# Attention, token mixer and gated mixer in one kernel: three engines in program order from batch 2 on, and the first token product behind the second channel product

## Chip, cores and metric

One core of one Trainium2 chip. The metric is the device time of one execution in microseconds (us). Engines: PE is TensorE, ACT is ScalarE, DVE is VectorE, POOL is GpSimd, SP is SyncE, which here only issues DMAs.

## The reference

Eight batches of 576 tokens, model width 512. Per batch:

```python
# attention in chunks of 64 tokens, 8 heads of 64
attn = softmax(q_c @ k_c.T / 8);  x = attn @ v_c            # x: 576 x 512
# token and channel mixer
u = x + (relu(x.T @ w_tok1) @ w_tok2).T                      # d_tok 256
x = u + relu(u @ w_ch1) @ w_ch2                              # d_ch 1536
# gated mixer
h = relu(x @ w_in);  a, v = h[:, :512], h[:, 512:]
v = (v - mean(v)) / sqrt(var(v) + 1e-6)                      # over features
out = (a * (w_spatial @ v + b_spatial)) @ w_out
```

## The kernel before

Each float32 operand is held as two float16 parts, a high one and the remainder ("hi" and "lo"), and each product is three products, hi x hi, hi x lo and lo x hi, in one PSUM accumulation. ScalarE rounds to the high part, VectorE or GpSimd subtracts for the remainder. That rounding, ReLU, residuals, statistics and softmax keep the other engines at work beside TensorE.

A batch `b` runs through these stages on TensorE: the first channel product (`ch1`, from batch 2 on `ch1_fast`), the second (`ch2`, from batch 3 on `ch2_fast`), the gate stage (`gate_v` for five token tiles and `gate` for four feature tiles, in turns), then for batch b+1 the token products `tok1` and `tok2`, then `gated`, the spatial product of batch b. The output projection `proj` of batch b is issued in the next batch, between pairs of the channel product. Attention of batch b+2 is put between all these in small steps: `at_steps` lists them for a group of 128 tokens (five groups a batch), `pump`, called after each matrix product, keeps a planned TensorE clock, and `a_step` runs the next step when a slower clock, scaled stage by stage with `PACES`, reaches its due time. `a_until(b + 1)` ahead of `tok1` runs what is left for batch b+1.

The fast channel products (batches 2 to 7, `ch1_fast`; 3 to 7, `ch2_fast`) are a Strassen-like form with seven block products in place of eight. The weight blocks and their sums are made once (`sum_steps`, batches 1 and 2), stored to HBM and streamed through 18 slots. `ch1_fast` goes in pairs p = 0 to 5; after each pair VectorE, ScalarE and GpSimd form seven operands `hF[p]` for the second channel product (lines 707 to 749). `ch2_fast` begins with `p1(0)`, `p1(1)`, `p2(0)`: `p2` adds to a PSUM bank that ScalarE must first have copied at L779.

PSUM is four buffers of two banks (`pm`), taken by every product in turn. `wrk` has three work tiles of 128 x 576.

The first part of the program, ahead of the loop over batches, has its order written out by hand. In the loop only TensorE's order is that of the program; ScalarE, VectorE, GpSimd and SP are ordered by the planner of the framework from its own cost estimates, with `tc.high_priority()` around the steps that are to come first. Each engine takes its instructions strictly in the order that results.

Of the kernel before, what the change touches and what calls it, by code (L numbers as in the profile page):

```python
# [1 line left out]

# [24 lines left out]
def mixer_kernel(ctx: ExitStack, tc, qk0, qk, v, wt1, wt2, wc1, wc2, win, wsp, bsp, wout, out):  # L27
# [10 lines left out]
    wrk = ctx.enter_context(tc.tile_pool(name="wrk", bufs=3))  # L38
# [4 lines left out]
    pm = ctx.enter_context(tc.tile_pool(name="pm", bufs=4, space=bass.MemoryType.PSUM))  # L43

# [176 lines left out]
    def at_steps(g):  # L221
# [12 lines left out]
        def score():  # L234
            m["sp"] = sp = pm.tile([128, 2, 512], F32, tag="m", name="mp")
            for h in range(4):
                for k, (x, y) in enumerate(THREE):
                    for r in range(2):
                        for c in range(nc_):
                            t = slice(64 * c, 64 * c + 64)  # L240
                            PE.matmul(out=sp[t, r, 64 * h:64 * h + 64], lhsT=qk16[half[r], x, 0, h, t],  # L241
                                      rhs=qk16[half[r], y, 1, h, t], start=(k == 0), stop=(k == 2))

        def shift():
            sc = m["sp"][rows, :, 0:256].rearrange("p r (h k) -> p r h k", k=64)
            mx = sm.tile([128, 2, 4, 1], F32, name="mx")
            m["sd"] = sd = sdp.tile([128, 4, 2, 64], F32, name="sd")
            DVE.tensor_reduce(out=mx[rows], in_=sc, axis=AX.X, op=ALU.max)
            DVE.tensor_tensor(out=sd[rows].rearrange("p h r k -> p r h k"), in0=sc,
                              in1=mx[rows].to_broadcast([n, 2, 4, 64]), op=ALU.subtract)  # L250
# [3 lines left out]

        def norm():
            sd = m["sd"][rows].rearrange("p h r k -> p (h r) k")
            mx = sm.tile([128, H, 1], F32, name="mx")
            DVE.tensor_reduce(out=mx[rows], in_=sd, axis=AX.X, op=ALU.add)
            DVE.tensor_scalar(out=mx[rows], in0=mx[rows], scalar1=1e-9, scalar2=None, op0=ALU.add)
            DVE.reciprocal(out=mx[rows], in_=mx[rows])  # L260
            DVE.tensor_tensor(out=sd, in0=sd, in1=mx[rows].to_broadcast([n, H, 64]), op=ALU.mult)  # L261
# [16 lines left out]
        def attend():  # L278
            m["av"] = av = pm.tile([128, 2, 512], F32, tag="m", name="mp")
# [25 lines left out]
        def x_lo():  # L305
# [3 lines left out]
        return [  # L309
            [lambda: at_load_qk(g)], [], [qk_hi], [qk_lo], [], [score],  # L310
            [lambda: wide_v(b, 2 * i, vals)],
            [shift], [], [expo], [norm, v_hi], [p_hi, v_lo], [p_lo], [], [], [attend], [x_out],
            [], [x_lo], [],
        ]


# [19 lines left out]
    def wide_steps(g):  # L336
# [11 lines left out]
        def score():  # L348
# [4 lines left out]
            m["sp"] = sp = pm.tile([128, 2, 512], F32, tag="m", name="mp")  # L353
# [33 lines left out]
        def attend():  # L387
            m["av"] = av = pm.tile([128, 2, 512], F32, tag="m", name="mp")
# [29 lines left out]
    KA, NA = 5, 20  # L418
    live = {}
    order = sorted((KA * g + s + 15 * (g >= 2 * NT), g, s) for g in range(NT, NG) for s in range(NA))  # L420
    todo = [0]

    def a_step():
# [4 lines left out]
        with tc.high_priority() if g < 2 * NT and s not in (0, 8) else nullcontext(), tc.issue_after(mark) if g < 2 * NT else nullcontext():  # L428
            for f in live[g][s]:
                f()  # L430

    def a_end(b):
        return [o[1:] for o in order].index((NT * b + NT - 1, NA - 1)) + 1
# [8 lines left out]
    pumps = []  # L442

    def pump(cols):
        t = cols / 2.4 + 2.5
        clock[0] += t
        slow[0] += t * pace[0]
        for p in pumps:
            while p[3]() and p[4][0] >= p[0]:
                p[2]()  # L450
                p[0] += p[1]
# [10 lines left out]
    def psum2():  # L462
        t = pm.tile([128, 2, 512], F32, tag="m", name="mp")
        return [t[:, 0, 0:288], t[:, 1, 0:288]], t[:, :, 0:288]

    def psum1():
        t = pm.tile([128, 2, 512], F32, tag="m", name="mp")
        return t[:, 0, :]
# [30 lines left out]
    def behind():  # L499
        stack = ExitStack()  # L500
        for ins in tail.values():
# [3 lines left out]
    PACES = ({"first": 0.2, "pair": 0.8, "ch1": 1.0, "ch2": 1.3, "gate": 1.0, "tok1": 1.0, "last": 0.3},  # L505
             {"first": 0.0, "pair": 0.2, "ch1": 1.0, "ch2": 1.95, "gate": 1.85, "tok1": 1.5, "last": 0.0})
# [7 lines left out]
    def first_sums(ps, m, x):  # L514
# [4 lines left out]
        split(x[:, m, s], xb[:, 0, m, s], xb[:, 1, m, s])  # L519
# [5 lines left out]
        if m == 3:  # L525
            q1, q2, q3 = sums[0], wrk.tile([128, 2, 288], F32, tag="t", name="q2"), wrk.tile([128, 2, 288], F32, tag="t", name="q3")
            DVE.tensor_tensor(out=q2, in0=b22, in1=q1, op=ALU.subtract)
            split(q2, tq[1][:, 0], tq[1][:, 1], POOL)
            DVE.tensor_tensor(out=q3, in0=b22, in1=b12, op=ALU.subtract)
            split(q3, tq[2][:, 0], tq[2][:, 1], POOL)  # L530
            DVE.tensor_tensor(out=q1, in0=b21, in1=q2, op=ALU.subtract)
            split(q1, tq[3][:, 0], tq[3][:, 1], POOL)
# [72 lines left out]
    def sum_steps(stage, p, room):  # L605
        rv = room.bitcast(F32)
        f = rv[:, 0:1024].rearrange("p (k m) -> p k m", k=4)
        s = rv[:, 1024:2048].rearrange("p (n k m) -> p n k m", n=4, k=2)
        g = room[:, 0:2048].rearrange("p (n e k m) -> p n e k m", n=4, e=2, k=2)
        if stage == 1:  # L610
            w = c1w[:, :, p]
            a11, a12, a21, a22 = f[:, 0:2, 0:128], f[:, 2:4, 0:128], f[:, 0:2, 128:256], f[:, 2:4, 128:256]
        else:
            w = c2w[:, :, 2 * p:2 * p + 2].rearrange("p e k (h m) -> p e (k h) m", h=2)
            a11, a12, a21, a22 = f[:, 0:2, 0:128], f[:, 2:4, 0:128], f[:, 0:2, 128:256], f[:, 2:4, 128:256]

        def join():
            DVE.tensor_tensor(out=f, in0=w[:, 0], in1=w[:, 1], op=ALU.add)
            for n, (k, c) in ((A11, (0, 0)), (A12, (2, 0)), (A22, (2, 128))):
                for e in range(2):  # L620
# [3 lines left out]
                    else:  # L624
                        at = (p // 2) * 512 + e * 256 + p % 2 * 128
                        SP.dma_start(out=c2s[:, n, :, at:at + 128].rearrange("q p m -> p q m"), in_=w[:, e, k:k + 2, c:c + 128])
# [12 lines left out]
        def low():  # L639
# [3 lines left out]
            else:  # L643
                at = (p // 2) * 512 + p % 2 * 128
                for q in range(2):
                    for e in range(2):
                        SP.dma_start(out=c2s[q, 3:7, :, at + e * 256:at + e * 256 + 128].rearrange("n p m -> p n m"), in_=g[:, :, e, q])

        return [join, first, second, high, low]
# [3 lines left out]
    def sum_next():  # L653
        with behind():
# [22 lines left out]
    def new_bank():  # L677
        return pm.tile([128, 2, 512], F32, tag="m", name="mp")

# [4 lines left out]

    def ch1_fast(full, between):
        high = tc.high_priority
        ab, cd = {}, {}

# [7 lines left out]
        def store(c, hi, lo, eng=POOL):  # L696
            ACT.activation(out=c, in_=c, func=AF.Relu)
            split(c, hi, lo, eng)

        for p in range(7):  # L700
            pace[0] = PACE["first" if p < 1 else "pair"]
            if p < 6:
                ab[p] = a = new_bank()
                product(a[:, 0], p, A11, xb[:, :, 0:2, T1], True)
                product(a[:, 1], p, S2, tq[1], True)
                with high():
                    ACT.activation(out=s1b[0], in_=a[:, 0, 0:288], func=AF.Copy)
                    DVE.tensor_tensor(out=u2b[p % 2], in0=a[:, 1, 0:288], in1=s1b[0], op=ALU.add)
            if p:
                d, u, xp = cd[p - 1], u2b[(p - 1) % 2], xs[(p - 1) % 2]  # L710
                product(d[:, 0], p - 1, S4, xb[:, :, 2:4, T2], False)
                product(d[:, 1], p - 1, A22, tq[3], False)
                with high():
                    c = new_work("c")
                    DVE.tensor_tensor(out=c, in0=d[:, :, 0:288], in1=spread(u), op=ALU.add)  # L715
                    if full:
                        f = hF[p - 1]
                        ACT.activation(out=xp[:, 1:4:2], in_=c, func=AF.Relu)
                        t13, t24 = new_work("t13"), new_work("t24")
                        relu_less = dict(scalar=0.0, op0=ALU.max, op1=ALU.subtract)  # L720
                        DVE.scalar_tensor_tensor(out=t13[:, 0], in0=c[:, 0], in1=xp[:, 0], **relu_less)
                        DVE.tensor_tensor(out=t24[:, 0], in0=xp[:, 2], in1=t13[:, 0], op=ALU.subtract)
                        DVE.scalar_tensor_tensor(out=t24[:, 1], in0=c[:, 1], in1=t24[:, 0], **relu_less)
# [430 lines left out]
```

## Time and profile before

| what | value |
|---|---|
| median of 3 runs | 1176.37 us (1174.98 to 1178.49) |
| profiled execution | 1176.0 us, span 1174.0 us |
| PE busy | 1100.7 us, 94% |
| DVE, ACT, POOL busy | 771.0, 501.8, 424.5 us |
| mean granted TensorE clock | 0.98 |

The span runs from the first to the last instruction of the profiled execution. Busy time is the union of an engine's instructions. A matrix product counts from its start to its modelled end, so products overlap and a busy TensorE isn't one at its peak. A releaser ("<-") is the instruction whose end let a waiting one start.

### The profile page before, as it was taken

The numbers are of one execution on the slowest core, as the hardware profiler recorded it, in microseconds if no ns is written. First come the engines' busy times: TensorE is split into PE (matmuls) and PEld (weight loads), VectorE is DVE, ScalarE is ACT, GpSimd is POOL, SyncE is SP. The second block draws the span as 40 slices with busy tenths as digits, with TensorE's granted clock in tenths as the row PEclk, the third lists the DMA queues.
The fourth block names the chain that finished last, engine by engine and source line by source line (L and its number), as shares of the span: only waits on it lengthen the run. The fifth ranks groups of instructions, "written<-read, shape, count | busy, mean of one in ns | idle before, by whom it ended". The sixth has DMA issues, their size and how long they took to land.

```text
span 1174.0 us, 26626 instructions
## 1 busy us (share of the span) xinstructions
PE 1100.7 (94%) x10860; PEld 774.0 (66%) x10860; DVE 771.0 (66%) x1299; ACT 501.8 (43%) x884; POOL 424.5 (36%) x392
## 2 busy tenths in 40 slices
PE   5898999999999999999799897998979999999998
PEld 4576757776577755766467574675746767677765
DVE  7999886765565487574666756667576675467342
ACT  3343444434345344453444634356243553346131
POOL 0000033352344445453335623346234452345221
PEclk9899999999999999999999998999989999999999
DMA  9488720654046442356514585145751469115401
GB/s 318 141 250 268 230 53 20 147 160 124 18 125 169 92 121 50 110 144 186 147 32 118 139 198 133 40 118 139 203 132 27 127 166 199 19 55 153 135 1 45
DMA packets 191819, 148.36 MB, mean 126 GB/s; under 512 B 107345, under 2 KB 175697, under 8 KB 189393
## 3 DMA queue, kind: packets, MB, share of 16 engines
q1 hardware_dynamic: 191696, 146.66, 45.8%
q8 instruction: 85, 1.39, 0.5%
q14 instruction: 38, 0.30, 0.1%
HBM read 112.00 MB, written 20.45 MB: 113 GB/s over the span
## 4 chain that ended last, share of the span: by engine, by line
PE 62%; DVE 20%; DMA 5%; ACT 5%; issue 3%; POOL 3%; SPq 1%; ACTq 0%; DVEq 0%; POOLq 0%
PE mp L669 23%; PE mp L457 22%; PE mp L939 5%; PE mp L862 4%; PE mp L836 3%; PE mp L480 3%; DVE gb L154 2%; DVE gb L150 1%; DMA qk<-in_qk 1%; DVE qk L232 1%; DVE gb L148 1%; DVE c L715 1%; PE mp L241 1%; DMA c2s<-vn 1%; DVE sd L261 1%
## 5 line engine op out<-in xcount | busy, mean ns | idle before, releaser
L669 PEld LDWEIGHTS <-c1w 128*128 128x128 f16 x2772 | 272.1, 99 | 94.3 <-issue 19.1
L669 PE MATMUL mp<-xb,c1w 128*128 128x288 f16 x864 | 127.4, 287 | 8.1 <-DVE c2w L749 6.7
L836 PE MATMUL mp<-hb,c2w 128*128 128x288 f16 x864 | 111.7, 288 | 4.2 <-DVE c2w L163 2.7
L457 PE MATMUL mp<-xb,inw 128*128 128x288 f16 x768 | 104.9, 296 | 9.5 <-ACT hb L921 8.9
L457 PE MATMUL mp<-spw,vn 128*128 128x288 f16 x896 | 111.6, 286 | 0.0
L457 PEld LDWEIGHTS <-inw 128*128 128x128 f16 x768 | 77.4, 101 | 38.0 <-issue 11.8
L457 PEld LDWEIGHTS <-vn 128*128 128x128 f16 x896 | 87.4, 98 | 22.8
L836 PEld LDWEIGHTS <-c2w 128*128 128x128 f16 x864 | 83.4, 99 | 27.5 <-DVE c2w L163 4.0
L669 PE MATMUL mp<-hb,c1w 128*128 128x288 f16 x630 | 91.8, 291 | 8.5 <-ACT vn L779 7.3
L939 PE MATMUL mp<-otw,gb 128*128 128x512 f16 x432 | 98.0, 379 | 0.0
L862 PE MATMUL mp<-inw,xb 128*128 128x512 f16 x384 | 91.6, 381 | 5.9 <-ACT xb L544 2.5
L669 PE MATMUL mp<-c2w,c1w 128*128 128x288 f16 x630 | 92.3, 292 | 0.0
L457 PE MATMUL mp<-xb,c1w 128*128 128x288 f16 x576 | 74.9, 290 | 4.4 <-DVE xb L538 2.5
L939 PEld LDWEIGHTS <-gb 128*128 128x128 f16 x432 | 42.3, 98 | 45.5
L457 PEld LDWEIGHTS <-c1w 128*128 128x128 f16 x576 | 56.2, 99 | 20.5 <-issue 2.9
L862 PEld LDWEIGHTS <-xb 128*128 128x128 f16 x384 | 36.1, 98 | 47.2 <-ACT xb L544 3.5
L669 PE MATMUL mp<-c1w 128*128 128x288 f16 x432 | 66.1, 288 | 0.0
L929 POOL TENSOR_TENSOR gb<-gt,gb 128x576 f16<-128x576 f32 x31 | 41.1, 1327 | 66.0 <-ACT gb L928 66.0
L545 POOL TENSOR_TENSOR xb<-rt,xb 128x576 f16<-128x576 f32 x7 | 11.7, 1676 | 140.3 <-ACT xb L544 140.3
L895 POOL TENSOR_TENSOR vn<-vt,vn 128x512 f16<-128x512 f32 x32 | 37.8, 1183 | 61.9 <-ACT vn L894 61.9
L269 POOL TENSOR_TENSOR p<-sd,p 128x512 f16<-128x512 f32 (+1 forms) x30 | 39.5, 1318 | 56.7 <-ACT p L266 54.8
L886 POOL TENSOR_TENSOR y<-z,mhalf 128x1 f32<-128x1 f32 (+1 forms) x40 | 24.1, 603 | 89.9 <-DVE z L885 86.2
(233 smaller groups left out, 1993.4 us busy)
## 6 DMA issues: line engine op xcount, KB each, us to landing
c1w<-c1s SPq DMA_DIRECT2D x252, 128.0 KB, 2.4
c1w<-c2s SPq DMA_DIRECT2D x210, 128.0 KB, 2.5
qk<-in_qk SPq DMA_DIRECT2D x96, 128.0 KB, 3.0
out<-o SPq DMA_DIRECT2D x31, 256.0 KB, 2.1
v<-in_v SPq DMA_DIRECT2D x56, 128.0 KB, 3.0
vn<-in_wc SPq DMA_DIRECT2D x4, 1024.0 KB, 4.9
otw<-in_wc SPq DMA_DIRECT2D x3, 1024.0 KB
spw<-in_wc SPq DMA_DIRECT2D x3, 1024.0 KB, 5.0
```

Source lines behind the costliest of these rows:

```text
L148: DVE.tensor_scalar(out=t, in0=w[:, :, 1], scalar1=3, scalar2=0x3FFFFFFF, op0=ALU.logical_shift_left, op1=ALU.bitwise_and)
L154: DVE.scalar_tensor_tensor(out=t, in0=w[:, :, 0], scalar=29, in1=t, op0=ALU.logical_shift_right, op1=ALU.bitwise_or)
L269: POOL.tensor_tensor(out=p_hl[rows, 1], in0=m["sd"][rows], in1=p_hl[rows, 0], op=ALU.subtract)
L457: PE.matmul(out=o, lhsT=l, rhs=r, start=(i == 0), stop=(i == len(seq) - 1))
L480: PE.matmul(out=pss[m], lhsT=l, rhs=r, start=(i + j == 0), stop=False)
L669: PE.matmul(out=o[:, 0:288], lhsT=w[:, a, k], rhs=b(e, k), start=(start and k + i == 0), stop=(stop and k == 1 and i == 2), skip_group_che ...
L836: PE.matmul(out=o, lhsT=c2w[:, a, k, mc], rhs=hb[:, k // 2, r, k % 2 * 2 + t], start=(k + e == 0), stop=(k == 11 and e == 2))
L862: PE.matmul(out=ps, lhsT=l, rhs=r, start=(k + e == 0), stop=(k == 3 and e == len(seq) - 1))
L886: POOL.tensor_tensor(out=y[0:n], in0=z[0:n], in1=mhalf[0:n], op=ALU.pow)
L895: POOL.tensor_tensor(out=vn[:, 2 * j + 1], in0=t, in1=vn[:, 2 * j], op=ALU.subtract)
L929: eng.tensor_tensor(out=gl, in0=t, in1=gh, op=ALU.subtract)
L939: PE.matmul(out=ps, lhsT=gb[:, l, k, tk], rhs=otw[:, r, k], start=(k == 0 and e == 0), stop=(k == 3 and e == 2))
```

## The change

From batch 2 on, ScalarE, VectorE and GpSimd also follow the order of the program (`ordered.enter_context`, `exact[0] = True`). SP stays with the planner. So that the program's order is usable, dependent steps are not issued where they stand but some microseconds of TensorE's planned clock later: `after(us, f)` pushes `f` on a heap, `tick` in `pump` runs what is due; ahead of batch 2 `after` runs `f` at once. `tok1` of batch b+1 moves from behind the gate stage to directly behind the second channel product of batch b (`next_tokens`), with attention of batch b+1 ended ahead of it and that of b+2 begun behind it; `tok2` stays. Attention's step list becomes times on one axis, ten units between groups; score and attend products wait for a minimum distance from the steps that feed them (`BEHIND`, `held`), and the pace table becomes three tables with other values. The sums for the second channel weights go from six whole to twelve half pieces, in `xs[0]`, spread over batch 2. A fifth projection moves into the first channel product, the gate tiles' order changes, `wrk` gets a fourth tile.

```diff
-    wrk = ctx.enter_context(tc.tile_pool(name="wrk", bufs=3))
+    wrk = ctx.enter_context(tc.tile_pool(name="wrk", bufs=4))
...
-        return [
-            [lambda: at_load_qk(g)], [], [qk_hi], [qk_lo], [], [score],
...
-        ]
+        return {0: lambda: at_load_qk(g), 4: qk_hi, 5.5: qk_lo, 10: score, 10.2: lambda: wide_v(b, 2 * i, vals), 11: top, 11.8: shift,
+                14: expo, 16: total, 17.5: norm, 18.8: v_hi, 19: p_hi, 19.8: v_lo, 20.5: p_lo, 28: attend, 29: x_out, 30.5: x_lo}
...
-    order = sorted((KA * g + s + 15 * (g >= 2 * NT), g, s) for g in range(NT, NG) for s in range(NA))
+    order = sorted((5 * g + s, g, s) for g in range(NT, 2 * NT) for s in range(20))
+    order += sorted((10 * g + s, g, s) for g in range(2 * NT, NG) for s in TIMES)
...
+    BEHIND = {10: (5.5, 3000.0), 28: (20.5, 7000.0)}
+
+    def a_open():
+        _, g, s = order[todo[0]]
+        if not exact[0] or s not in BEHIND:
+            return True
+        s0, gap = BEHIND[s]
+        return not held[0] and clock[0] >= told[g, s0] + gap
...
+    def after(us, *fs):
+        for f in fs:
+            if exact[0]:
+                heappush(jobs, (clock[0] + 1000 * us, after.count, f))
+                after.count += 1
+            else:
+                f()
...
-    PACES = ({"first": 0.2, "pair": 0.8, "ch1": 1.0, "ch2": 1.3, "gate": 1.0, "tok1": 1.0, "last": 0.3},
-             {"first": 0.0, "pair": 0.2, "ch1": 1.0, "ch2": 1.95, "gate": 1.85, "tok1": 1.5, "last": 0.0})
+    SPAN = 102000.0
+    PACES = ({"first": 0.2, "pair": 0.8, "ch1": 1.0, "ch2": 1.3, "gate": 1.0, "tok1": 1.0, "last": 0.3, "turn": 0.8},
+             {"first": 0.0, "pair": 1.1, "ch1": 1.0, "ch2": 1.7, "gate": 1.2, "tok1": 1.0, "last": 0.0, "turn": 0.9},
+             {"first": 0.0, "pair": 0.7, "ch1": 1.0, "ch2": 1.75, "gate": 1.45, "tok1": 1.0, "last": 0.0, "turn": 0.3})
...
+            after(0.7, second)
+            after(1.3, lambda: put(xp[:, 2:4], 1))
+            after(1.6, others)
+            after(3.0, lambda: put(t13, 3))
+            after(3.6, lambda: put(t24, 5))
...
+        start = 0.8 if j < 4 else 2.2
+        after(start, spread_of)
+        after(start + 2.0, newton)
+        if exact[0]:
+            after(start + 2.2, finish)
+            return None
         return finish
...
+            if b == FIRST_FAST:
+                ordered.enter_context(tc.manual_schedule(engines={ET.Activation, ET.DVE, ET.Pool}))
+                exact[0] = True
+                sum_pump([(2, p, q) for p in range(6) for q in range(2)], 1550.0)
...
+            def next_tokens():
+                a_until(b + 1)
+                pumps[:] = pumps[1:]
+                pace[0] = PACE["tok1"]
+                last = tok1()
+                attention_from(b + 2, 0.0, 112000.0 if b < 1 else SPAN)
+                return last
+
+            if exact[0] and b < B - 1:
+                next_tokens()
```

In `sums_of` (new, called after each pair) the five `after` lines place the sums and splits of lines 721 to 727; `put` is ScalarE's rounding and GpSimd's remainder. `others` holds the sums of lines 723 and 724. The residuals' copies (`tail_copy`), `first_sums`, `gated` and the half tile of `gate_v` get `after` in the same way.

## Rows read from the trace of the kernel before

**Rows 1.** windows, batches 2 to 6: stretch, us, engines' busy us, clock, DMA share, GB/s

```profile
337.30:477.90 140.60, 135.80 (x1278) 94.92 (x1276) 85.27 (x138) 61.17 (x109) 68.77 (x68) 0.99 0.42 108
477.90:623.10 145.20, 133.98 (x1326) 93.11 (x1324) 93.37 (x167) 65.61 (x120) 60.77 (x53) 0.95 0.47 125
623.10:769.60 146.50, 134.79 (x1338) 93.41 (x1337) 94.59 (x167) 66.49 (x123) 60.28 (x53) 0.97 0.49 126
769.60:913.50 143.90, 132.52 (x1327) 92.24 (x1325) 94.60 (x167) 65.49 (x120) 60.89 (x53) 0.96 0.48 126
913.50:1046.50 133.00, 129.91 (x1243) 91.13 (x1242) 82.93 (x151) 59.98 (x115) 56.54 (x51) 1.00 0.47 115
```

**Rows 2.** windows: channel 2, gate (batch 4), gate (6), channel 2 (7)

```profile
668.00:705.40 37.40, 35.12 (x422) 26.86 (x421) 21.15 (x37) 13.46 (x24) 13.47 (x13) 0.95 0.74 181
705.40:740.80 35.40, 28.51 (x322) 17.07 (x320) 23.65 (x50) 15.56 (x27) 11.58 (x14) 0.90 0.50 129
...
993.00:1017.70 24.70, 24.70 (x246) 15.62 (x246) 14.85 (x39) 11.18 (x21) 10.10 (x12) 1.00 0.31 46
...
1087.90:1118.70 30.80, 30.80 (x253) 24.61 (x252) 9.11 (x19) 4.91 (x10) 7.72 (x8) 1.00 0.39 117
```

**Rows 3.** waits of TensorE, whole span: us in total, times, longest

```profile
PE mp L241 <- ACT vt L872: 9.1, 3, 3.6
PE mp L457 <- ACT hb L921: 8.9, 3, 3.1
...
PE mp L669 <- ACT vn L779: 7.3, 4, 2.3
PE mp L669 <- DVE c2w L749: 6.7, 3, 2.2
PE mp L457 <- ACT hb L487: 3.9, 8, 2.1
...
PE mp L862 <- ACT xb L544: 2.5, 2, 1.8
...
PE mp L862 <- DVE xb L545: 1.6, 2, 1.4
```

**Rows 4.** timeline of TensorE, batch 4: start, us, instructions, idle before

```profile
674.83 1.31 PE L669 MATMUL mp<-hb,c1w 128*128 128x288 f16 x9 [2.28 <-ACT vn L779]
675.93 2.36 PE L669 MATMUL mp<-c2w,c1w 128*128 128x288 f16 x9
...
730.85 4.60 PE L457 MATMUL mp<-xb,inw 128*128 128x288 f16 x24 [2.69 <-ACT hb L921]
735.28 2.75 PE L862 MATMUL mp<-inw,xb 128*128 128x512 f16 x12
737.87 3.10 PE L457 MATMUL mp<-xb,inw 128*128 128x288 f16 x24
```

**Rows 5.** timeline of VectorE, batch 4, turn between the channel products

```profile
667.20 1.48 DVE L261 TENSOR_TENSOR sd<-sd,mx 128x512 f32<-128x512 f32 x1
668.61 0.74 DVE L715 TENSOR_TENSOR c<-mp,vn 128x576 f32<-128x576 f32 x1
```

**Rows 6.** timeline of ScalarE, batch 3, gate stage

```profile
585.05 0.63 ACT L894 ACTIVATE vn<-vt 128x512 f16<-128x512 f32 x1 [3.06 <-DVE vt L891]
585.58 0.63 ACT L921 ACTIVATE hb<-mp 128x576 f32<-128x576 f32 x1
```

**Rows 7.** groups by line, VectorE: count, busy us, mean ns, idle before

```profile
L724 DVE TENSOR_TENSOR t<-vn 128x288 f32<-128x288 f32 x15 | 16.4, 1096 | 0.0
...
L749 DVE SCALAR_TENSOR_TENSOR c2w<-mp,c2w 128x288 f16<-128x288 f32 x15 | 6.7, 444 | 0.0
```

**Rows 8.** DMA issues; columns: count, median us to landing

```profile
x<-xh SPq DMA_TRANSPOSE x24, 3.3
```

**Rows 9.** groups by line, GpSimd

```profile
L306 POOL TENSOR_TENSOR xh<-xT,xh 128x512 f16<-128x512 f32 x24 | 28.1, 1170 | 42.8 <-ACT xh L303 23.8 <-PE mp L241 9.1 <-issue 9.0
```

More of the change, by code (lines that the diff above doesn't have):

```diff
@@ L234, in score @@
         def score():
[L235 removed]
+            m["sp"] = sp = bank()
             for h in range(4):
@@ L447, in pump, with tick @@
         slow[0] += t * pace[0]
+        tick()
+    def tick():
+        while jobs and jobs[0][0] <= clock[0]:
+            heappop(jobs)[2]()
         for p in pumps:
@@ L644, in low @@
                 at = (p // 2) * 512 + p % 2 * 128
[L645 to L649, printed above, removed]
+                for e in range(2):
+                    SP.dma_start(out=c2s[q, 3:7, :, at + e * 256:at + e * 256 + 128].rearrange("n p m -> p n m"), in_=g[:, :, e])
+        return [join, first, second, high, low] + [lambda: None] * (stage > 1)
     todo_sums = []
     def sum_next():
-        with behind():
+        with nullcontext() if exact[0] else behind():
             todo_sums.pop(0)()
@@ L992, in mixer_kernel, with when @@
         wticks[0] = KW * 5 + 1
-    with tc.manual_schedule(engines={mybir.EngineType.PE}):
+    with tc.manual_schedule(engines={ET.PE}), ExitStack() as ordered:
         def attention_from(b, skip, span):
             if b < B:
-                end = a_end(b)
-                pumps.append([slow[0] + skip, span / (end - todo[0]), a_step, lambda: todo[0] < end, slow])
+                end, base, first = a_end(b), slow[0] + skip, order[todo[0]][0]
+                unit = span / (order[end - 1][0] - first)
+                def when():
+                    at = [order[min(i, end - 1)][0] for i in (todo[0] - 1, todo[0])]
+                    return max(base + (at[1] - first) * unit, slow[0] + (at[1] - at[0]) * unit * 0.6)
+                pumps.append([base, span / (end - todo[0]) if b < 3 else when, a_step, lambda: todo[0] < end and a_open(), slow])
         def held_tick():
@@ L1023, in mixer_kernel @@
                 full = b >= FIRST_FULL
-                places = (1, 3, 5, 6) if full else (2, 5)
-                early, pend = pend[:len(places)], pend[len(places):]
-                ch1_fast(full, {k: (lambda i=i: proj(b - 1, i)) for k, i in zip(places, early)})
-            pace[0] = PACE["ch2"]
+                ch1_fast(full, {k: (lambda i=i: proj(b - 1, i)) for k, i in zip((5, 2, 4, 1, 3), pend)})
+                pend = []
+            pace[0] = PACE["ch2" if b < FIRST_FULL else "turn"]
             if b == 0:
@@ L1074, in mixer_kernel @@
             if b < B - 1:
-                a_until(b + 1)
-                pumps[:] = pumps[1:]
-                pace[0] = PACE["tok1"]
-                last = tok1()
-                attention_from(b + 2, 0.0, 112000.0)
+                if not exact[0]:
+                    last = next_tokens()
                 if b == 0:
@@ L1094, in mixer_kernel @@
                 pend = list(range(5 if b % 2 else 4))
-        banks = [t[:, a] for t in [pm.tile([128, 2, 512], F32, tag="m", name="mp") for _ in range(3)] for a in range(2)]
+        settle()
+        banks = [t[:, a] for t in [bank() for _ in range(3)] for a in range(2)]
         for ks in ((0, 1), (2,)):
```

256 lines of the change are left out of this document (137 added, 119 removed).

## The prediction

> **What bounds the kernel now.** I read the batches first, as stretches of the trace cut at the end of each batch's spatial product [rows 1]. TensorE is the busiest engine in every batch, so time is lost where it stops or runs slowly. Batches 3, 4 and 5 take 145.2, 146.5 and 143.9 us, batch 6 takes 133.0 with about as many matrix products. The reader is to see that the long ones have less PE share and a granted clock of 0.95 to 0.97, where batch 6 has 1.00, and that no other engine is near full: VectorE, the next one, has 94.6 of 146.5 us.
>
> The stages of batch 4 [rows 2] say where. The second channel product takes 37.4 us against 30.8 us in batch 7, where there is no attention beside it. The gate stage takes 35.4 us against 24.7 us in batch 6, where TensorE never stops. VectorE is busy 23.65 us in the long gate stage and 14.85 us in the short one: the difference is attention.
>
> Then the waits of TensorE [rows 3]. Few kinds make up nearly all from batch 2 on, and they come at the same places of each batch: a score product waits for a PSUM bank that ScalarE empties (9.1 us), a gate product for the next bank (8.9), the second channel product for ScalarE's copy of its first sum (7.3), a first channel product for VectorE's remainder (6.7), `tok2` for the hidden layer of `tok1` directly ahead of it (3.9), the gate stage for the last residual (2.5 and 1.6).
>
> The timeline of TensorE [rows 4] shows what a wait costs beyond itself. Behind the 2.28 us wait that ends at 674.8 us nine products take 1.31 us, and then the next nine 2.36; behind the wait that ends at 730.9 us 24 take 4.60 us, and the next such 24 take 3.10. The clock column of [rows 2] is 0.95 and 0.90 in just these stages, so part of them ran at the lower of the two levels, 1.2 GHz.
>
> Last, the engines that are waited for. At 667.2 us VectorE runs a normalisation of attention (1.48 us) while the channel sums of the last pair, which begin at 668.6 us, stand behind it [rows 5]; ScalarE's copies for those sums come late, and the short copy that TensorE needs stands behind them. In the gate stage ScalarE waits 3.06 us with the rounding of `vn` at the head of its queue, for a VectorE result, and only then does the 0.63 us that empties a bank for TensorE [rows 6]. So TensorE waits not for capacity but for work that is in the wrong place in an in-order queue.
>
> **The change part by part.** *Order of three engines.* No arithmetic goes away. `after` puts a dependent step later in program text by a time on TensorE's planned clock: the remainders, Newton steps and roundings no longer stand ahead of the copies that free a bank. `finish` of a gate tile comes 3.0 us after its product, while the next gate product is 24 x 0.123 = 2.9 us long [rows 4], so the emptying of that bank stands ahead of it in ScalarE's queue. The wait of [rows 6] has no place there. In the turn from the first to the second channel product the last split is put 3.6 us later, behind the first copy.
>
> What can be won is the sum of the waits that the order makes [rows 3]:
> - gate stage, 9.1 + 8.9 = 18.0;
> - turn into the second channel product, 7.3;
> - inside the first channel product, 6.7;
> - residual to gate, 2.5 + 1.6 = 4.1;
> - `tok1` to `tok2`: 3.9 in eight waits, the longest 2.1, so the others about 0.26; three of those lie ahead of batch 2, which leaves 3.1.
>
> That is 39.2 us. A wait also costs the filling of the array: nine products take 1.31 us, which is eight distances of 0.123 us and one of 0.3, so about 0.17 is lost at each of some 22 waits, 3.7 us. The slow clock is bounded from both sides. From below: two slow stretches a batch in 3, 4 and 5 and two in batch 2, eight at the 1.5 us of 4.60 against 3.10, 12 us. From above: one minus the clock times the length of batches 2 to 5 [rows 1], 1.4 + 7.3 + 4.4 + 5.8 = 18.9, which counts the waits themselves as slow. I take 13, near the lower end, as the rows 4 are direct. All together 56 us, at most 62.
>
> How much is kept? The residual wait and the `tok2` wait I count as gone (7.2): the first is at most 1.8 us long [rows 3] and gets 28 products of 512 columns as cover, 6 us by the 2.75 us for twelve [rows 4]; the second gets the whole gate stage between. If that cover is gone, the same 7.2 us come back. Gate waits: VectorE had 8.8 us of attention there, and the pace of attention in this stage goes from 1.85 to 1.45, so 14.85 + 6.9 = 21.7 us of VectorE work meet 24.7 us of TensorE. That is 88%, too close to lose no time in a fixed order; a quarter stays, 4.5 us. Of the turn and the first channel product (14.0) a sixth stays, 2.3. Of filling and clock (16.7) a sixth, 2.8.
>
> *`tok1` behind the second channel product.* It asks for two PSUM buffers while the last two of the channel product are being emptied. No row shows this wait; below it is nothing, above it is 1.8 us a batch (the longest wait for that residual), and below nothing it can't be, as a bank is never freed earlier by it. Nearest is the wait of 0.26 us; I take 0.2 us, 1.0 for five batches. What is late next is `tok1` itself, if attention isn't through (rival four).
>
> *Attention.* 17 steps in place of 20, ten units from group to group, paced so that it ends before the second channel product does; its products are held until 3.0 and 7.0 us behind the steps that feed them. Its loads and transposes move with it on SP's queue, whose order the planner still chooses; I count nothing, between a gain and a loss of 0.5 us a batch. *Sums for the second channel weights*: spread over batch 2 in twelve halves. 48 small GpSimd instructions in place of 24; even if each new one cost the 1.17 us of a full tile [rows 9], GpSimd would rise from 68.8 to 97 us in a batch of some 130 [rows 1]: hidden. *Fifth projection* moved into the first channel product and a fourth work buffer: nothing, same products, no wait in [rows 3] on either. Batches 0 and 1 are still planned; their planned order shifts a little, nothing within 2 us.
>
> Sum: 55.9 - 4.5 - 2.3 - 2.8 - 1.0 = 45.3 us. The profiled execution took 1176.0 us around a span of 1174.0, and the median of the runs is 1176.37, so one is as good as the other: **1131 us**.
>
> **Rivals.** *One: everything is recovered.* 1176 less 56 to 62, 1114 to 1120; I count below 1116. For it: batch 6 runs at clock 1.00 under the old order already. Against: it has less attention.
>
> *Two: VectorE and GpSimd hold each other.* The same VectorE difference of two SBUF operands takes 1.10 us on average, a form with one PSUM operand 0.44 us [rows 7]. The hand order puts splits on GpSimd at fixed times (1.3, 3.0, 3.6 us) and the sums between (0.7, 1.6). If four sums a pair each lose 0.66 us, a pair needs 2.6 us more of VectorE; with two pairs of a batch that have no projection to hide it, that is 5 us in each of five batches, 25 us given back, and the time is 1156; with one such pair 1144. Against: the 1.6 us sums come before the first split can start. The Trainium skill (SBUF — State Buffer, Who interferes with whom) says that a VectorE instruction with two SBUF inputs contends with a GpSimd one that reads SBUF and that the second to issue waits for the whole of the first. By that rule it would be about 1156; the 1.10 us rows agree with it, though no row shows which engine came first.
>
> *Three: transfers bind.* The second channel product streams weights at a DMA share of 0.74 in 37.4 us; in 33 us that is 0.84 [rows 2]. If late weights hold the stage at its old length in batches 3 to 6, the turn's 7.3 us and four slow stretches (6.0) aren't won: 1144. Against: 0.84 is under 1 and the stage starts with 18 slots loaded.
>
> *Four: attention isn't ready for `tok1`, slower than before.* `tok1` used to come behind the gate stage; now all five groups must be in token order by the end of the second channel product. A last group that is still at its normalisation owes 1.5 us [rows 5], two GpSimd steps of 1.2 [rows 9], two transposes of 3.3 [rows 8], its products (some 0.6) and two copies of 0.6 [rows 6]: 12.3 us with TensorE idle, five times 62 us, 1176 - 45 + 62 = 1193. It decides from 9 us a batch. Against: the plan has 24.7 x 1.45 in the gate, 53.9 in the second channel product (30.8 x 1.75) and about 19 in the first, 109 units for a span of 102, so it ends some 4 us early.
>
> *Five: the planner's order was this one already.* Then 1176. Against: [rows 5, 6] show an order with the remainder ahead of the copy.
>
> **How the numbers follow.** Forecast (1116 to 1142) 0.58; rival one 0.08; two, beyond 1142, 0.16; three 0.05; four 0.08; five 0.05. The range from 1114 to 1158 leaves out about 0.02 below, four, five and the tail of two above: 0.2. A measurement of this kernel tells 0.3%, 3.5 us, from no change. Faster is the forecast with one, two and three, 0.87; same is five, 0.05; slower is four, 0.08.
>
> **What would show it.** Batches 3 to 5 at 129 to 135 us with a clock of 0.99 or more; no wait of `tok2` for the hidden layer; waits for ScalarE in the gate under 5 us in sum; gate stage at 25 to 27 us behind `tok1`. Wrong it is if TensorE waits at the first `tok1` product for tokens or banks, if the VectorE sums of the channel pairs get longer, or if waits for weights appear in the second channel product.

## The result, and the profile after

| | before | after |
|---|---|---|
| median of 4 runs | 1177.38 us | 1156.55 us (1155.12 to 1159.56) |
| ratio | | 0.9829, interval 0.9802 to 0.9856 |
| profiled execution | 1176.0 us, span 1174.0 | 1157.5 us, span 1155.7 |

The change is worth 21 us. The forecast was 1131 with a range from 1114 to 1158: the time is inside the range, at its upper end, and less than half of the forecast gain came. Below, times of other kernels are set against these medians; the kernel before, run beside each group of experiments, had medians of 1176.9 to 1178.5, and each ratio is against the one beside it.

Batches 2 to 6 after, windows with the columns of [rows 1], cut at the same product:

```profile
337.50:482.80 145.30, 136.68 (x1471) 96.46 (x1470) 99.10 (x166) 68.19 (x125) 74.17 (x89) 1.00 0.49 120
482.80:620.70 137.90, 130.21 (x1327) 91.40 (x1325) 96.34 (x171) 63.40 (x122) 61.40 (x55) 0.99 0.50 134
620.70:762.00 141.30, 132.70 (x1337) 93.03 (x1336) 93.87 (x168) 64.66 (x122) 61.47 (x51) 0.99 0.50 131
762.00:898.90 136.90, 130.01 (x1327) 91.69 (x1325) 94.87 (x168) 64.41 (x123) 62.18 (x55) 0.99 0.51 133
898.90:1028.20 129.30, 128.30 (x1146) 90.69 (x1144) 79.38 (x146) 57.72 (x111) 58.54 (x51) 1.00 0.40 110
```

Against [rows 1] the batches change by +4.7, -7.3, -5.2, -7.0 and -3.7 us, -18.5 in sum. The PE column splits that. TensorE's idle time, length less busy time, goes from 42.2 to 32.8 us, and its busy time from 667.0 to 657.9: 9.4 us fewer of standing still and 9.1 of running slowly, although the five stretches hold 96 products more than in [rows 1]. The forecast had 31.4 (39.2 less 4.5, 2.3 and 1.0) and 13.9. So the clock did most of its part; the standing still did not go away.

Why, the waits of TensorE after show (us in total, times, longest):

```profile
PE mp L295 <- DMA pT<-p: 13.5, 6, 4.2
...
PE mp L520 <- DMA x<-xht: 5.8, 4, 3.0
...
PE mp L712 <- DVE vn L774: 3.0, 7, 1.5
PE mp L924 <- ACT xb L582: 2.5, 1, 2.5
...
PE mp L712 <- ACT vn L840: 2.2, 2, 1.1
PE mp L245 <- ACT o L1022: 2.0, 1, 2.0
...
PE mp L712 <- DVE t L846: 1.3, 2, 0.7
PE mp L493 <- ACT hb L990: 1.1, 1, 1.1
...
PE mp L493 <- ACT hb L523: 0.8, 3, 0.3
```

The two gate waits of [rows 3] for ScalarE, 18.0 us, are gone, and so is the first channel product's for the remainder, 6.7 us; of the turn's 7.3 us 2.2 are left (L840). The two rows with DMA have taken their place: attention's attend product (L295) and `tok1` (L520) wait for DMA transposes, ten times, 19.3 us, all of it in batches 2 to 5. The kernel before had neither row.

The second channel product, `tok1` and the gate stage of batch 4, windows; the first and the last row answer to [rows 2]:

```profile
665.80:709.40 43.60, 36.96 (x542) 28.14 (x540) 24.91 (x45) 17.26 (x33) 17.66 (x16) 0.96 0.74 189
709.40:717.30 7.90, 6.17 (x30) 2.73 (x28) 2.43 (x5) 0.87 (x2) 1.88 (x2) 1.00 0.76 207
717.30:742.40 25.10, 25.10 (x249) 15.65 (x248) 18.88 (x38) 12.35 (x22) 8.76 (x9) 1.00 0.38 75
```

The gate stage runs without a stop, 25.1 us where it had 35.4, with 73 products fewer. The second channel product is 6.2 us longer than before and idle for 6.6, with 120 more products in it; `tok1` behind it is idle for 1.7.

The long wait of this stage, on TensorE's timeline:

```profile
698.15 1.27 PE L712 MATMUL mp<-hb,c1w 128*128 128x288 f16 x9
...
704.30 0.51 PE L295 MATMUL mp<-pT,v 64*64 64x64 f16 x24 [4.15 <-DMA pT<-p]
...
705.44 2.37 PE L712 MATMUL mp<-hb,c1w 128*128 128x288 f16 x9
```

Nine products that take 1.27 us ahead of it take 2.37 behind it: the granted clock of the stage is 0.96, so part of it ran at 1.2 GHz. What the transpose waited for, first GpSimd's timeline:

```profile
691.57 1.16 POOL L314 TENSOR_TENSOR xh<-xT,xh 128x512 f16<-128x512 f32 x1 [2.51 <-ACT xh L311]
692.68 1.15 POOL L277 TENSOR_TENSOR p<-sd,p 64x512 f16<-64x512 f32 x1
```

and SyncE's (SPq: the DMA issues of its queue, start and time taken):

```profile
689.63 0.66 SPq L335 DMA_DIRECT2D v<-in_v  x1
690.38 2.37 SPq L632 DMA_DIRECT2D c1w<-c2s  x2
692.79 0.63 SPq L335 DMA_DIRECT2D v<-in_v  x1
693.51 1.49 SPq L632 DMA_DIRECT2D c1w<-c2s  x3
695.10 0.49 SPq L222 DMA_DIRECT2D qk<-in_qk  x1
695.68 0.54 SPq L632 DMA_DIRECT2D c1w<-c1s  x1
696.27 1.13 SPq L222 DMA_DIRECT2D qk<-in_qk  x2
697.50 1.00 SPq L632 DMA_DIRECT2D c1w<-c1s  x2
698.55 0.47 SPq L222 DMA_DIRECT2D qk<-in_qk  x1
699.12 0.54 SPq L632 DMA_DIRECT2D c1w<-c1s  x1
699.75 1.27 SPq L315 DMA_TRANSPOSE x<-xh  x1
701.11 1.25 SPq L278 DMA_TRANSPOSE pT<-p  x1
702.45 1.02 SPq L632 DMA_DIRECT2D c1w<-c1s  x2
```

The operand `p` is complete at 693.83 us, and its transpose leaves at 701.11, 7.3 us later; `xh` is complete at 692.73 and leaves at 699.75. In between SyncE issues without a pause: the thirteen rows add up to 12.86 of the 13.8 us from 689.63 to 703.47. Over the whole second channel product of batch 4, its rows add up to some 39 of 43.6 us, where before had some 32 of 37.4. SyncE appears in no line of busy time, so nothing on the profile's page says that it is full.

### The profile page after: what moved, and what is told of

The parts are those of the page before. It is cut to its first block, busy times and chain, and to the rows that moved or that the text cites. A ratio compares the mean times of both kernels' runs of the same rounds, so it can differ in the third digit from the quotient of the medians.

```text
span 1155.7 us, 26608 instructions
## 1 busy us (share of the span) xinstructions
PE 1090.7 (94%) x10860; PEld 771.9 (67%) x10860; DVE 772.0 (67%) x1311; ACT 496.0 (43%) x890; POOL 440.1 (38%) x416
## 4 chain that ended last, share of the span: by engine, by line
PE 36%; DVE 11%; DMA 4%; ACT 4%; POOL 3%; issue 3%; SPq 1%; ACTq 0%; DVEq 0%; POOLq 0%
PE mp L712 19%; PE mp L493 6%; PE mp L1012 5%; PE mp L924 3%; DMA pT<-p 2%; DVE xb L558 1%; DVE qk L236 1%; PE mp L516 1%; DMA x<-xht 1%; DVE vt L954 1%; DVE e L950 1%; DVE st L943 1%; POOL y L947 1%; DVE xT L555 1%; PE mp L295 1%
## 5 line engine op out<-in xcount | busy, mean ns | idle before, releaser
L493 PE MATMUL mp<-xb,inw 128*128 128x288 f16 x768 | 99.0, 286 | 0.0
L493 PEld LDWEIGHTS <-inw 128*128 128x128 f16 x768 | 74.8, 98 | 23.8
L947 POOL TENSOR_TENSOR y<-z,mhalf 128x1 f32<-128x1 f32 (+1 forms) x40 | 29.7, 743 | 124.0 <-DVE z L946 124.0
L1012 PEld LDWEIGHTS <-gb 128*128 128x128 f16 x432 | 42.2, 98 | 45.2
L236 DVE TENSOR_TENSOR qk<-qk,qk 128x1024 f16<-128x1024 f32 (+1 forms) x30 | 38.4, 1280 | 36.3 <-ACT qk L233 36.1
L673 POOL TENSOR_TENSOR xs<-xs 128x128 f32<-128x128 f32 x12 | 11.6, 967 | 114.7 <-DVE xs L661 114.7
```

The costliest lines, as they stand in the source:

```text
L236: DVE.tensor_tensor(out=qk16[:, 1, :, :, rows], in0=qk32[:, :, :, rows], in1=qk16[:, 0, :, :, rows], op=ALU.subtract)
L493: PE.matmul(out=o, lhsT=l, rhs=r, start=(i == 0), stop=(i == len(seq) - 1))
L673: POOL.tensor_tensor(out=s[:, 0], in0=a21, in1=a22, op=ALU.add)
L947: POOL.tensor_tensor(out=y[0:n], in0=z[0:n], in1=mhalf[0:n], op=ALU.pow)
L1012: PE.matmul(out=ps, lhsT=gb[:, l, k, tk], rhs=otw[:, r, k], start=(k == 0 and e == 0), stop=(k == 3 and e == 2))
```

## The experiments

Four theories. A: the planner's order on SyncE puts transposes too late. B: attention's products stand too close behind the steps that feed them. C: `tok1` comes too early in its new place. D: SyncE's issue time is used up in the second channel product, whatever its order.

**SyncE in program order too** (A).

```diff
-tc.manual_schedule(engines={ET.Activation, ET.DVE, ET.Pool})
+tc.manual_schedule(engines={ET.Activation, ET.DVE, ET.Pool, ET.SP})
```

> SyncE's queue is put in program order too from batch 2 on, beside the three engines; nothing else changes. Theory A (the order of SyncE's queue, still the planner's, puts attention's transposes behind weight-slot loads that wait for TensorE): the waits of TensorE for transposed probabilities (13.5 us in the changed kernel) and for transposed tokens at tok1 (5.8) fall together below 5 us, and the time comes to 1130 to 1142 us. Theory B (the distance between the probabilities' remainder and the attend product is too short, whatever SyncE does): both waits stay above 12 us in sum, 1150 to 1162. Theory C (tok1 comes too early for attention): the token wait stays at about 6, the other may fall, 1140 to 1150.

1175.35 us, ratio 0.9978 (0.9955 to 1.0): the whole gain is lost. The waits for `pT` rise to 18.8 us, those for `x` to 9.7. SyncE's timeline, where GpSimd was through with `p` at 704.52:

```profile
698.29 3.86 SPq L632 DMA_DIRECT2D c1w<-c2s  x8
702.25 2.75 SPq L632 DMA_DIRECT2D c1w<-c1s  x4
705.09 2.40 SPq L222 DMA_DIRECT2D qk<-in_qk  x4
707.54 1.30 SPq L335 DMA_DIRECT2D v<-in_v  x2
708.94 1.27 SPq L315 DMA_TRANSPOSE x<-xh  x1
710.30 1.22 SPq L278 DMA_TRANSPOSE pT<-p  x1
```

Again a queue without gaps, and a transpose 5.8 us late. The planner's order was better than the program's, so A falls in this form. An order that puts each transpose ahead of loads not needed yet was not run: four of the issues between 693.83 and 701.11 us of the kernel after are weights of the next batch's first product (`c1s`).

**Attend held 12 in place of 7 us behind its remainder** (B).

```diff
-    BEHIND = {10: (5.5, 3000.0), 28: (20.5, 7000.0)}
+    BEHIND = {10: (5.5, 3000.0), 28: (20.5, 12000.0)}
```

> The attend product is held until 12.0 us of TensorE's planned clock behind the remainder of the probabilities, in place of 7.0. Theory A: the lateness of 4 to 7 us on SyncE is covered, so the wait for transposed probabilities falls from 13.5 to under 4 us, but the last group ends later ahead of tok1, so that the wait for tokens grows from 5.8 to 10 to 20: 1150 to 1165 us. Theory B: the same fall of the first, the second grows less than 4: 1138 to 1146. Theory C: the token wait grows by 5 us a batch, 25 in sum: 1165 to 1180.

1180.13 us, ratio 1.0018 (1.0003 to 1.0033). There are five waits for `pT` in place of six, but they add up to 38.8 us, the longest 9.6; that for `x` is gone. All five stand at the last, half group of a batch (24 products), which `a_until` by the code issues ahead of `tok1` without the distance; the other groups no longer wait. So the distance covers the late transposes where there is room for it, but it moves the end of the chain against `tok1`, and as a remedy it falls.

**`tok1` back behind the gate stage** (C).

```diff
-            if exact[0] and b < B - 1:
-                next_tokens()
...
-                if not exact[0]:
-                    last = next_tokens()
+                last = next_tokens()
```

> Program order stays, but the first token product and the end of attention go back behind the gate stage, where they were before the change. Theory C: token and probability waits vanish together (under 2 us), residual waits of about 4 us and tok2 waits of about 3 us return, 1135 to 1145 us. Theories A and B: the wait for transposed probabilities stays above 9 us, the token wait may fall, residual and tok2 waits return: 1152 to 1165.

1161.85 us, ratio 0.9861 (0.9829 to 0.9893), 5 us slower than after. The waits for `x` are gone, but those for `pT` are 17.3 us, and `tok2` waits 3.8 us for its hidden layer again. The new place of `tok1` isn't the cause of the larger part; the expected 1135 to 1145 us for theory C is missed.

**Attend without the transpose of `p`** from batch 3 on; attention then uses old probabilities.

```diff
+            if b < 3:
-            SP.dma_start_transpose(out=pT[:, :, rows], in_=...)
+                SP.dma_start_transpose(out=pT[:, :, rows], in_=...)
```

> The transposes of the probabilities are left out for batches 3 to 7 (attention of these batches multiplies old probabilities): it measures what these transposes and the waits for them cost. Theories A and B: the 13.5 us of waits go but for those of batch 2, with two or three slow-clock stretches of 1.7 us and the filling of the array, and tok1 gets its tokens earlier: 1132 to 1142 us. Theory C: the token wait stays near 5 us, 1140 to 1147.

1144.07 us, ratio 0.9715 (0.9676 to 0.9754): 12 us faster than after, about the 13.5 us of the wait. Waits for `x` remain, 10.5 us. The edit takes the issues of these transposes off SyncE as well, so it gives the price of the part and not its cause.

**The move of `tok1` alone, on the kernel before.**

```diff
+            if b >= FIRST_FAST and b < B - 1:
+                a_until(b + 1); ...; last = tok1(); attention_from(b + 2, 0.0, 112000.0)
```

> The kernel before with one part of the change alone: the first token product, and with it the end of attention for its batch, directly behind the second channel product from batch 2 on; engines' order stays the planner's. The sum of the prediction gives residual and tok2 waits, 7.2 us: 1165 to 1171. Theory C (attention isn't ready so early): the waits for tokens and scores rise, 1177 to 1200.

1164.62 us, ratio 0.9893 (0.9849 to 0.9938): 12 us of gain from this part alone. It brings the new wait with it, for `x` 8.5 us, while the score product's wait for ScalarE (9.1 us in [rows 3]) is gone.

Next, D by dose: **fewer issues for the same bytes.** The three 128 KB pieces of a weight block of the second channel product are loaded as one of 384 KB, in the kernel after and in the kernel before:

```diff
+            if stage == 2:
+                if streamed[0] + 3 > upto:
+                    break
+                at = streamed[0] % SLOTS * 512
+                SP.dma_start(out=call[:, at:at + 1536], in_=c2s[p, n])
+                streamed[0] += 3
+                continue
...
```

> The three weight pieces of one block product of the second channel product are loaded by one transfer of 384 KB in place of three of 128 KB: 28 issues fewer on SyncE's queue in each such stage, the same bytes, on top of the change. Theory D (SyncE's queue is full in the second channel product: about 38 weight issues of 0.4 to 0.5 us, 15 attention loads of 0.6 and 6 transposes of 1.27 us against some 38 us, so transposes leave it late): SyncE's queue is busy under 28 us in that stage, the lag from GpSimd's remainder to the transpose falls from 4 to 7 us to under 3, the waits for transposed probabilities and tokens from 19.3 to under 8 us, time 1134 to 1145. Theory B (the chain of attention on VectorE, ScalarE and GpSimd is late by itself): the waits stay above 14, 1150 to 1160.

> The same joined weight loads in the kernel before, without the change. Theory D: no wait of TensorE in the kernel before was for a transpose, so nothing moves: 1172 to 1181. The rival (joined loads are better by themselves, by fewer and longer packets): 1160 to 1170.

After: 1147.2 us, ratio 0.9738 (0.9691 to 0.9786), single runs from 1141.0 to 1151.4; in the profiled execution, the one of 1141.0, waits for `pT` 6.2 and for `x` 3.8 us. Before: 1168.51, ratio 0.9929 (0.9898 to 0.9959); "no change" was wrong, and the time lies where the expectation had put the rival, that joined loads gain by fewer and longer packets. What moved is the score product's wait for ScalarE (9.1 us in [rows 3]), which fell to 4.1, and the transfers of others did not get faster: loads of q and k of 128 KB landed in a median of 3.0 us before and 2.9 with joined loads there, 2.9 and 3.4 in the kernel after.

**The loads of q, k and v from ScalarE's queue**, so that SyncE keeps weights and transposes.

```diff
-                SP.dma_start(out=qk32[half[r], s, :, 0:n],
+                (ACT if exact[0] else SP).dma_start(out=qk32[half[r], s, :, 0:n],
...
```

> On top of the change the loads of q, k and v for attention are issued from ScalarE's queue in place of SyncE's from batch 2 on, with the same bytes and positions in the program. Theory D: six issues of about 0.6 us a group leave SyncE's queue, 3.6 us of some 13 a group; the lag of the transposes falls below 4 us, waits for them to 8 to 12 us, time 1140 to 1150. Theory B: waits unchanged, and ScalarE, which now spends those 3.6 us, is later: 1156 to 1166.

1168.96 us, ratio 0.9930 (0.9903 to 0.9958). Both ranges of the expectation are missed. In the attention of batches 4 to 7 the transposes of `p` leave at most 0.9 us behind GpSimd's remainder (up to 7.3 in the kernel after), and the waits for `pT` fall to 8.4 us, of which 5.2 is one wait in batch 2. But there is a new one: the second channel product waits 12.5 us for ScalarE's copy (L840). ScalarE's timeline and TensorE's at the longest of these waits:

```profile
812.30 5.11 ACTq L335 DMA_DIRECT2D v<-in_v  x2
817.46 0.68 ACT L748 ACTIVATE vn<-c 128x576 f32<-128x576 f32 x1 [7.76 <-DMA x<-xh]
...
818.76 0.39 ACT L840 ACTIVATE vn<-mp 128x288 f32<-128x288 f32 x1
```

```profile
819.20 2.32 PE L712 MATMUL mp<-hb,c1w 128*128 128x288 f16 x9 [3.96 <-ACT vn L840]
```

ScalarE stands for 7.76 us among these issues, by the profile until a transpose of tokens has landed, although one issue for `v` takes only a median of 0.63 us: what holds up a load holds up all that stands behind it in that queue, and here TensorE waits for that. So SyncE is relieved, and ScalarE pays.

**More issues for the same bytes**: each 128 KB piece as two loads of 64 KB, 42 more issues a batch, after and before.

```diff
+            if stage == 2:
+                for c in (0, 256):
+                    SP.dma_start(out=slot(streamed[0])[:, c:c + 256], in_=src[:, c:c + 256])
...
```

> The opposite of the joined loads, on top of the change: each weight piece of the second channel product is loaded by two transfers of 64 KB, so that SyncE issues 42 more in each such stage, the same bytes. Theory D (SyncE's issue time is what makes attention's transposes late): the waits for transposed probabilities and tokens grow from 19.3 us to over 40 us, time 1175 to 1205. Theory B (distance too short, chain late by itself): the waits stay within 5 us of 19.3, 1154 to 1164.

> The same split loads in the kernel before, without the change. If the planner's attention is far enough ahead of its products, the waits of TensorE grow by less than half of what they grow with the change: 1178 to 1192. If SyncE's queue binds both alike, as the 8.5 us won by joined loads in the kernel before make possible: 1195 to 1215.

After: 1203.98 us, ratio 1.0223 (1.0169 to 1.0277), 56.3 us of waits for `pT`. Before: 1204.82, ratio 1.0234 (1.0183 to 1.0285), and there too TensorE now waits for `pT`, 33.1 us: with more issues the old places of attention no longer hide the queue. The second channel product of the first of the two, as a window, and a part of it on SyncE's timeline:

```profile
679.50:733.70 54.20, 38.32 (x543) 28.85 (x541) 26.74 (x46) 17.35 (x33) 19.05 (x17) 0.87 0.61 155
```

```profile
689.76 12.52 SPq L634 DMA_DIRECT2D c1w<-c2s  x23
702.38 2.42 SPq L222 DMA_DIRECT2D qk<-in_qk  x4
```

23 issues of 64 KB take 12.52 us, 0.54 each, and the DMA engines are less busy than after (0.61 against 0.74) while TensorE waits; SyncE's rows add up to some 53 of the 54.2 us. What binds is the number of issues, not the bytes.

**Both channel products' loads joined**, two or three pieces in one. The blocks of the first product are stored in the order of their use, so that neighbours can be joined: some 33 weight loads a batch in place of 84 (14 and 19 for 42 and 42).

```diff
+    PLACE = {A11: 0, S2: 1, S4: 2, A22: 3, S1: 4, S3: 5, A12: 6}
...
-            SP.dma_start(out=slot(streamed[0]), in_=src)
-            streamed[0] += 1
+            SP.dma_start(out=call[:, i % SLOTS * 512:(i % SLOTS + w) * 512], in_=src)
+            streamed[0] += w
```

> Joined loads for both channel products on top of the change: the weight blocks of the first are stored in the order of their use and loaded two or three at a time, so that a batch's 84 weight issues become about 34. Theory D: the lag of the transposes falls below 2 us and the waits for them below 5 us, 1132 to 1144. Theory B: no further fall below the 10 us that were left with joined loads of the second product alone, 1142 to 1150.

1136.02 us (1133.32 to 1137.71), ratio 0.9649 (0.96 to 0.9698): faster than both kernels, 20.5 us below after. Its waits, and its second channel product of batch 4 with batches 3 to 5 as windows:

```profile
PE mp L295 <- DMA pT<-p: 5.5, 8, 1.7
...
PE mp L520 <- DMA x<-xht: 1.6, 2, 1.0
```

```profile
653.50:692.00 38.50, 35.39 (x543) 27.33 (x541) 24.37 (x44) 15.23 (x29) 16.14 (x14) 1.00 0.94 220
477.20:608.50 131.30, 128.40 (x1327) 90.90 (x1325) 95.74 (x171) 63.31 (x122) 61.57 (x55) 1.00 0.56 142
608.50:743.90 135.40, 131.04 (x1339) 92.21 (x1337) 94.78 (x168) 64.67 (x122) 61.52 (x51) 1.00 0.52 134
743.90:874.80 130.90, 128.37 (x1327) 90.89 (x1325) 94.71 (x168) 64.38 (x123) 62.17 (x55) 1.00 0.56 139
```

The stage of 43.6 us takes 38.5, at the full clock, with the DMA engines at 0.94: they were not what had been full. The three batches take 18.5 us less than after, 13.4 of it idle time and 5.1 busy time.

**Joined, with attend held 9 us and attention's span shortened to 94** (does distance remain?), **joined on the kernel before, and joined with `tok1` back.**

> The kernel with both joined loads, with the attend product held until 9.0 in place of 7.0 us behind the remainder of the probabilities, and the span over which attention is paced shortened from 102 to 94 so that it doesn't end later. If with SyncE's queue relieved the 7.0 us distance is what is left (theory B for the rest): waits for probabilities under 2 us, time 5 to 10 us below the kernel with joined loads. If not: the same or slower by up to 8 us.

1148.81 us, ratio 0.9751 (0.9709 to 0.9793), 13 us slower than joined alone, more than the 8 that were expected at most; waits for `pT` 7.9, of which 5.9 is one in batch 2, and `x` 6.8. Two numbers were changed at once, so which of them costs the time isn't shown; as a remedy, more distance falls here too.

> The kernel before with both joined loads. It gives the worth of the change once SyncE's queue is relieved on both sides, against the 1136.0 us of the change with joined loads. If the orders of ScalarE, VectorE and GpSimd are what holds the kernel before (the prediction's reason): its waits for ScalarE and VectorE in the gate, the turn and the first channel product stay above 20 us, the time stays at 1162 to 1172, and the change is worth 26 to 36 us there. If SyncE's queue was what held the kernel before too: 1140 to 1155, and the change is worth under 20 us.

1162.03 us, ratio 0.9857 (0.9815 to 0.9898). In this order the gate product still waits 7.9 us for ScalarE, the second channel product 8.3 and the first 6.7, 22.9 us in all, as expected if the orders of the three engines held it; the score product's wait is gone.

> The change with both joined loads, but the first token product back behind the gate stage. With the queue relieved, theory C (tok1 comes too early) would have this faster than 1136: 1125 to 1133. The prediction's sum has residual and tok2 waits return, 7 us: 1141 to 1147.

1138.05 us, ratio 0.9664 (0.9633 to 0.9694). Its runs (1135.9 to 1139.4) and those with `tok1` in the new place overlap: about 2 us, where 5 had been measured without joining. Neither expected range holds.

## Why the prediction was wrong, point by point

**The step that failed** is the one on attention's loads and transposes: that they move with it "on SP's queue, whose order the planner still chooses; I count nothing, between a gain and a loss of 0.5 us a batch". Measured, the attend product and `tok1` waited 19.3 us for them in batches 2 to 5, 4.8 us a batch, with the lower clock behind the longer waits on top; joining the loads gives back 20.5 us and ends at 1136, 5 us from the forecast. The prediction counted operations on SyncE's queue as work for a planner to order. It never added up their time, although the trace of before has the same prices, here on SyncE's timeline in the second channel product of batch 4:

```profile
674.94 6.48 SPq L594 DMA_DIRECT2D c1w<-c2s  x11
682.31 1.29 SPq L270 DMA_TRANSPOSE pT<-p  x1
```

The old places of attention's products hid the queue at that number of issues. Before, each attend product began 12 to 95 us behind the end of its remainder on GpSimd; after, 18 of 30 begin 3 to 11 us behind it (starts and ends in the two timelines). With 3.3 us for the transpose [rows 8], a delay of 7 us then shows.

That it is the number of issues is shown by the dose: 42 more a batch cost 47 us, 28 fewer bring 9, some 51 fewer 20.5, always with the same bytes. In the attention of batches 4 to 7 the transpose of `p` left at most 11.5, 5.0 and 2.7 us behind its operand in these three, and 7.3 after. From issue to landing it took a median of 3.1, 3.2 and 3.2 us, and 3.2 after: what changes is the time ahead of the issue, not the transfer, so fewer and longer packets aren't the cause. Taking the transpose of `p` out brings 12, and moving loads to ScalarE's queue moves the delay there. The Trainium skill (DMA: Bandwidth & Descriptors, Issuing engines are not separate DMA queues) says that issuing from several engines saves only the sequencer's time to start a DMA, which is usually small beside the DMA itself. For one load the rows agree, 0.54 us from one issue to the next and a median of 2.5 us to landing; their sum, though, was what TensorE waited for.

**The terms that were won.** *Gate waits*: 18.0 forecast less 4.5; from batch 2 on no gate product waits for ScalarE any more, and no score product for the gate's copies. In batch 2 a score product waits 2.0 us for a projection's copy (L1022) and `tok2` 1.1 for the gate's (L990, which was L921). The fear of a VectorE too full for a fixed order was too large. *Turn and first channel product*: 14.0 less 2.3; 2.2 is left of these two. But a sum of VectorE in the first channel product (L774), which no row of before waits for, now costs 3.0 us, and the second channel product waits 1.3 for a residual (L846). *Residual and `tok2`*: 7.2 forecast; the three `tok2` waits for the hidden layer that are left are those ahead of batch 2, so that part is right. Of the residual's 4.1, a wait of 1.8 and one of 0.2 lay ahead of batch 2 as well, where the change does nothing, and could not be won; there it is one wait of 2.5 now. *Filling and clock*: 16.7 less 2.8, measured 9.1 in busy time; with the joined loads, 5.1 more come in batches 3 to 5 alone. That the rest of the term was held by the new waits is an inference from this. *`tok1` behind the second product*: no wait for a bank; the move is worth 12 us on the kernel before and 5 in the kernel after.

**The rivals.** *Two* (VectorE and GpSimd in each other's way) gave 1156, which is what was measured, by a cause that doesn't carry it: VectorE's busy time is 772.0 us against 771.0, and no wait of TensorE names those sums of the channel pairs. That the time lies in the range at all is luck, as its upper end stood for this rival. Their difference of two SBUF operands (L724 in [rows 7], now L754) takes about a microsecond as before, 32.8 us in all where it had 26.7, but the four sums together fell from 87.9 to 76.8:

```profile
L754 DVE TENSOR_TENSOR t<-xs 128x288 f32<-128x288 f32 x15 | 18.0, 1199 | 0.0
L754 DVE TENSOR_TENSOR t<-vn 128x288 f32<-128x288 f32 x15 | 14.8, 989 | 0.0
```

*Three* (late weights): no row of waits for weights, and the DMA share of that stage stayed at 0.74. Its 1.00 as the limit was the wrong scale; the queue that starts the transfers was the scale. *Four* (attention not ready for `tok1`) is near: its place and its transposes are right, but its cause isn't the steps of the last group, and the price is 5.8 us in all for `x`, not 62; a wait of `tok1` for tokens is a sign of being wrong that the prediction itself names. The larger part, 13.5 us, is at attend. *One* (below 1116) and *five* (1176) are far off.

**How much belongs to the change.** Joined loads win 16 us in the kernel before too (1178.5 to 1162.0). There late loads of q and k were seen only as a score product that waited for ScalarE, which [rows 3] names. ScalarE itself waited for them, here in the gate stage of batch 4, before:

```profile
716.72 1.06 ACT L229 ACTIVATE qk<-qk 128x1024 f16<-128x1024 f32 x1 [6.51 <-DMA qk<-in_qk]
```

These waits of ScalarE add up to 26.4 us before and to 5.5 with joined loads, where the score product's 9.1 us are gone. So part of what the prediction put down to the order of ScalarE was SyncE's. The change itself is worth 21 us with SyncE full and 26 (1162.0 to 1136.0) with it relieved.

**Open.** Batch 2 got 4.7 us longer: TensorE is busy 0.9 us more and idle 3.8 more. Of its 193 products more than in [rows 1], 192 are score and attend products, drawn forward; batch 6 has 97 products fewer. Whether that made the new waits there was not tested. An order of SyncE with the transposes first was not run. Why the joined second product scatters by 10 us between runs wasn't found. What follows at a DMA share of 0.94 wasn't tried.

## What to carry to other kernels

A queue that issues DMAs in order is an engine: ahead of moving a consumer closer to its DMA, add up the issues of that stage, number times duration, as for VectorE; the page's busy time leaves them out. Where it was full here, joining loads helped; the program's order, more distance and ScalarE's queue, each as it was tried, did not. When an order is tightened, ask of every transfer whose lateness the slack had hidden what stands ahead of it.

## What the runs showed of the hardware

The time of an issue hardly follows the size. The instruction of a weight load took a median of 0.38 us of SyncE at 64, 128 and 384 KB, and one behind another they came every 0.54 us (23 of 64 KB in 12.52 us). That of a DMA transpose took a median of 1.27 in the kernel after; in the joined kernel, at a DMA share of 0.94, one took 3.91. A load of 384 KB landed in a median of 3.5 us, one of 128 KB in 2.5. Issued from ScalarE, a load of q or k took about as long as from SyncE, a median of 0.61 against 0.59 us; at the longest wait, what cost time was that ScalarE's next instruction stood behind a load that had to wait.
